# Memory-augmented segment attention with a routed MLP: another layout for the left rows' outputs, and their x loaded at another place

## The chip, the cores and the metric

One Trainium2 chip, one of its cores. The metric is the device time in microseconds of one launch. The core has a matrix engine (TensorE, "PE" in the profile, its weight loads "PEld"), VectorE (DVE), ScalarE (ACT), GpSimd (POOL) and SyncE (SP). SP issues the streamed weights; GpSimd issues the small transfers.

## The reference

What is computed, cut to what matters (2048 rows of 1024, 32 heads of 128, 8 memory rows, 64 segments of 32 rows):

```python
xn = _layernorm(A_x)
mem = A_mem0
for s in range(64):
    h = concat([mem, xn[:, s*32:(s+1)*32]])            # 8 + 32 = 40 rows
    q, k, v = h @ Wq, h @ Wk, h @ Wv                   # 32 heads of 128
    p = softmax(where(mask, q @ k.T * scale, -1e9))    # memory columns, or causal
    o = (p @ v) @ Wo
    mem = o[:, :8]                                     # goes to the next segment
    outs.append(o[:, 8:])
out = x + concat(outs) + B(xn)                         # B: xn plus a gated MLP on 2 routed rows
```

Each segment needs the memory of the one before, so the 64 segments run one after the other.

## The kernel before, in words

**Rows.** A segment has 40 rows: 8 memory rows and 32 of x. The 32-row "main" tile holds the first 24 rows of x and the 8 memory rows. The last 8 rows of x of each segment, the **left rows**, do not depend on the memory, so four segments' left rows (a group of 32) are projected together, one group ahead, in "passes" that use a weight block while it is in SBUF for the main rows. `PASSES` and `COPIES` say by hand in which segment of four (j = s mod 4), phase and step each pass and each copy of a finished unit stands; the unit "o" (the left rows' output projection, tile WL) runs from phase 6 of j = 3 into the start of the next j = 0.

**A segment.** Six phases p of eight steps kc (query, key, query, key of the two halves of 16 heads, then the two halves of the values), each with four matmuls a step (line 780); then 16 steps w of the output projection (`project`, line 578). `hook(p, kc, f)` puts f behind step (p, kc); hooks of one step run in the order in which they were registered, and the copies of `COPIES` are registered first. The order of instructions on each engine is that of the program (`manual_schedule`). `transposes` turns queries and keys and makes QT and KT (lines 633 to 640), `scores` (lines 643 to 663), `exponent` and `soften` (lines 667 to 683) do the softmax of a half, `attend` (lines 686 to 708) multiplies with the values and copies the main rows' result to OT (line 706) and the left rows' to OTL (line 708).

**Weights.** 44 of the 64 blocks of 512 KB stay in SBUF; 20 are streamed each segment through five slots (line 356). A slot is given back when the block's last use in the segment is issued.

**OTL.** One tile a group, [128, 4 segments, 8 rows, 32 heads]. While j is under 3, its part for j = 3 also serves as the zero-filled scratch of the softmax of the left rows (`zeros_and_left`, cleared by `clear_pl`, line 721, on GpSimd). For j = 3 the scratch is the first half of the 512-wide buffer with the tag "bx".

**The left rows' x** is needed twice, loaded by `load_left` (line 323, four transfers of 16 KB on GpSimd's queue). In j = 0 it is loaded for the next group at (3,0) into OTL's part 1, normalised at (5,3) (`norm_left`, line 328) and turned at w = 8. In j = 3 it is loaded for this group at (2,0) into the second half of "bx", made into x + xn at (3,6) (`sum_left`, lines 330 to 337) and added by TensorE at the start of unit "o" (line 556).

**Other users of the tags.** "bx" also holds a block brought back from PSUM (`bring_back(0)`, w = 11, used in phase 0), the left rows' result OL (`copy_unit`, line 598, stored by line 601) and their queries and keys on the way to DRAM; "vl1" holds the left rows' values of the second half.

**GpSimd's queue** in a segment: four stores of the segment before (line 853), the clearing of the scratch, four loads of the next segment's x (`load_seg`, line 275, at (2,0)), in j = 0 four stores of OL, in j = 0 and 3 four loads of left rows, one load of the left rows' queries and keys (line 485, w = 9).

Of the kernel before, what the change touches and what calls it, by code (L numbers as in the profile page):

```python
# [8 lines left out]
BF16 = mybir.dt.bfloat16  # L9
# [43 lines left out]
def kernel(  # L53
# [219 lines left out]
    def load_seg(s):  # L273
        for g in range(4):
            nc.gpsimd.dma_start(out=X[s % 2][32 * g:32 * g + XM, :],  # L275
                                in_=x2[s * SEG:s * SEG + XM, 256 * g:256 * (g + 1)])
# [43 lines left out]
    def load_left(G, t):  # L320
        o4 = x2[4 * G * SEG:4 * (G + 1) * SEG, :].rearrange("(s r) d -> s r d", s=4)
        for g in range(4):
            nc.gpsimd.dma_start(out=t[32 * g:32 * (g + 1), :], in_=o4[:, XM:SEG, 256 * g:256 * (g + 1)])  # L323
        return t
# [185 lines left out]

    def left_out():
        if "otl" not in group:
            group["otl"] = one.tile([P, 4, XL, H], BF16, tag="otl", name="OTL")
        return group["otl"]

    VL = {}
# [63 lines left out]
                                 stop=(last and hs == 1), tile_position=(0, 32 * g), skip_group_check=True)  # L580

    def lhs_left(h):
        return otl_of[0][:, :, :, h].rearrange("p s r -> p (s r)")

    xl_of, otl_of = [None], [None]

    def copy_unit(u, s, engine):
        PS, n = units.pop(u)
        assert n == 0, (u, s, n)
        Gu = group_of(u, s)  # L590
        copy = nc.scalar.copy if engine == "scalar" else nc.vector.tensor_copy
        half = int(u[-1]) if u != "o" else 0
        if u[0] == "v":
            VL[half] = one.tile([P, 512], BF16, tag=f"vl{half}", name="VL")
            copy(out=VL[half][:, :], in_=PS[:, :])
        elif u == "o":
            OL = one.tile([P, 256], BF16, tag="bx", name="OL")
            copy(out=OL[:, :], in_=PS[:, 0:256])
            o4 = out2[4 * Gu * SEG:4 * (Gu + 1) * SEG, :].rearrange("(s r) d -> s r d", s=4)
            for g in range(4):  # L600
                nc.gpsimd.dma_start(out=o4[:, XM:SEG, 256 * g:256 * (g + 1)], in_=OL[32 * g:32 * (g + 1), :])
        else:
            XBl = one.tile([P, 512], BF16, tag="bx", name="XBl")
            copy(out=XBl[:, :], in_=PS[:, :])
            stores.append(lambda: nc.scalar.dma_start(out=ql_d[Gu][2 * half + "qk".index(u[0])], in_=XBl[:, :]))
            if engine == "scalar":
                stores.pop()()

    for s in range(NSEG):
# [9 lines left out]
        def hook(p, kc, fn):  # L619
            hooks.setdefault((p, kc), []).append(fn)  # L620

        def transposes(mat, half, XB):
            PTq = PTB.rearrange("p (i j r) -> p i j r", i=4, j=4)
            for il in range(4):
                nc.tensor.transpose(out=PTq[:, il, :, :].rearrange("p j r -> p (j r)"), in_=XB[:, il * P:(il + 1) * P],  # L625
                                    identity=IDENT[:, :])
            pv = PTq.rearrange("p i j r -> p (i j) r")
            with_left = s > 0 and mat == 0 and half == 0
            if with_left:
                turn_lx()  # L630
            if mat == 0:
                QT[half] = one.tile([P, 16, 32], BF16, tag="bE", name="QT")
                nc.scalar.copy(out=QT[half][:, :, :], in_=pv)  # L633
                if with_left:
                    new_qkl()
            else:
                KT[half] = one.tile([P, 16, NK], BF16, tag="kt", name="KT")
                nc.scalar.copy(out=KT[half].rearrange("p (i q) k -> p i q k", i=4)[:, :, :, 32:NK],
                               in_=qkl[0][:, :, 2 * half + 1, :, :])
                nc.vector.tensor_copy(out=KT[half][:, :, 0:32], in_=pv)  # L640

        def scores(half):
            QKL = qkl[0]
# [25 lines left out]
        def soften(half):  # L669
            S8 = SPS.rearrange("p i a k -> p (i a) k")  # L670
            DN = one.tile([P, 8], F32, tag="nm", name="DN")
            nc.vector.tensor_reduce(out=DN[:, :], in_=S8, axis=AX.X, op=ALU.add)
            nc.vector.reciprocal(out=DN[:, :], in_=DN[:, :])
            PT2 = one.tile([P, 2, 4, 64], BF16, tag=("bA", "bE")[half], name="PT2")
            PTm, PTl = PT2[:, 0], PT2[:, 1]
            PM = PTl.rearrange("p i q -> p (i q)").rearrange("p (b k) -> p b k", b=8)
            PLt = zeros_and_left().rearrange("p (b k) -> p b k", b=8)
            dnb = DN[:, :].unsqueeze(2)
            nc.vector.tensor_tensor(out=PM, in0=S8[:, :, 0:32], in1=dnb.to_broadcast([P, 8, 32]), op=ALU.mult)
            nc.vector.tensor_tensor(out=PLt[:, :, XL * j:XL * (j + 1)], in0=S8[:, :, 32:NK],  # L680
                                    in1=dnb.to_broadcast([P, 8, XL]), op=ALU.mult)
            nc.vector.transpose(out=PTm.rearrange("p i q -> p (i q)"), in_=PM.rearrange("p b k -> p (b k)"))
            nc.vector.transpose(out=PTl.rearrange("p i q -> p (i q)"), in_=PLt.rearrange("p b k -> p (b k)"))
            PTs[half] = (PTm, PTl)

        def attend(half, ph, turn_too=None):
            if half not in OT:
                OT[half] = one.tile([P, 4, 4, SEG], BF16, tag=("kt", "bC")[half], name="OT")
                if half == 0:
                    nxt["wo"] = psA.tile([P, 512], F32, tag="acc", name="WO")  # L690
                sums[half] = [BS[:, 0:4 * NK] if half else nxt["wo"][:, 256:256 + 4 * NK], OPB]
            PTm, PTl = PTs[half]
            for il in range(4):
                for jl in range(2):
                    q0 = 32 * (2 * ph + jl)
                    o = sums[half][jl][:, il * NK:(il + 1) * NK]
                    nc.tensor.matmul(o, lhsT=VM[half][q0:q0 + 32, il * P:(il + 1) * P], rhs=PTm[q0:q0 + 32, il, 0:NK],  # L697
                                     start=True, stop=False, tile_position=(q0, 0), skip_group_check=True)
                    nc.tensor.matmul(o, lhsT=VL[half][q0:q0 + 32, il * P:(il + 1) * P], rhs=PTl[q0:q0 + 32, il, 0:NK],
                                     start=False, stop=True, tile_position=(q0, 0), skip_group_check=True)  # L700
            if turn_too is not None:
                turn_too()
            for jl in range(2):
                ov = sums[half][jl].rearrange("p (i q) -> p i q", i=4)
                copy = nc.scalar.copy if half == 0 or jl == 0 else nc.vector.tensor_copy
                copy(out=OT[half][:, 2 * ph + jl, :, :], in_=ov[:, :, 0:SEG])
                h0 = 16 * half + 8 * ph + 4 * jl
                copy(out=left_out()[:, j, :, h0:h0 + 4].rearrange("p r i -> p i r"), in_=ov[:, :, SEG:NK])

        def zeros_and_left():
            return nxt["bx"][:, 0:256] if j == 3 else left_out()[:, 3].rearrange("p r h -> p (r h)")

        def clear_pl():
            if j == 3:
                nxt["bx"] = one.tile([P, 512], BF16, tag="bx", name="BX")
            z = zeros_and_left()
            if j in (1, 2):
                z = z.rearrange("p (b k) -> p b k", b=8)[:, :, XL * (j - 1):XL * j]  # L720
            nc.gpsimd.memset(z, 0.0)

        def get_left():
            if j == 3:
                nxt["xl"] = load_left(G, nxt["bx"][:, 256:512])
            else:
                nxt["xl"] = load_left(G + 1, left_out()[:, 1].rearrange("p r h -> p (r h)"))

        def prep_left():
            if j == 0:  # L730
# [28 lines left out]
        hook(3, 4, exponent)  # L759
        hook(3, 4, lambda: soften(0))  # L760
        if s + 1 < NSEG:
            hook(2, 0, lambda: load_seg(s + 1))
        if j == 3 or (j == 0 and G + 1 < NT):
            hook(4 if s == 0 else 2 if j else 3, 0, get_left)
            hook(*((3, 6) if j == 3 else (5, 3)), prep_left)
        hook(4, 6, lambda: scores(1))
        hook(5, 0, exponent)
        hook(5, 0, lambda: soften(1))
# [3 lines left out]
        for p, (mat, half) in enumerate(PHASES):  # L772
# [24 lines left out]
            if mat < 2:  # L797
# [2 lines left out]
                hooks.setdefault((p + 1, 3), []).insert(0, lambda m=mat, h=half, b=XB: transposes(m, h, b))  # L800

                if s == 0:
                    XBl = (left_out()[:, 1:3].rearrange("p s r h -> p (s r h)") if mat == 0 else
                           one.tile([P, 512], BF16, tag=("bA", "vl1")[half], name="XBl")[:, :])
                    nc.scalar.copy(out=XBl, in_=PSl[:, :])
                    hooks[p + 1, 3].insert(0, lambda m=mat, h=half, b=XBl: turn_first(m, h, b))
                    nc.gpsimd.dma_start(out=ql_d[0][2 * half + mat], in_=XBl)
# [170 lines left out]
```

## Time and profile before

| | |
|---|---|
| median of 3 runs | 1936.07 us (1923.14 to 1949.76) |
| the profiled execution, time | 1945.1 us |
| the profiled execution, span | 1943.5 us |
| busy: PE, PEld, DVE, ACT, POOL | 1595.4, 891.1, 898.0, 700.3, 440.5 us |
| moved by DMA | 712.42 MB, mean 367 GB/s |
| streamed weights | 1134 transfers of 512 KB, 63 of 256 KB |

How to read the rows: a group's row gives line, engine, operation, what it writes and reads with shapes, the count, then busy us and mean ns of one, then the engine's idle time just before and what ended it. A row of the timeline gives start and duration in us, engine, line, operation, count, and in brackets the idle time before it and what ended that. A row of windows gives the stretch, its length, each engine's busy time with its instructions, the granted TensorE clock (1.00 is full speed), the mean busy share of the 16 DMA engines (packets of a queue can overlap, so it can pass 1) and GB/s. The view of one line lists what its engine waited for in front of it: total us, times.

### The profile page before, as it was taken

The page shows a single profiled execution, that of the slowest core. Times are in us where ns is not written, and L with a number is a line of the kernel's source. Part 1 is how long each engine was busy: PE and PEld are TensorE (multiplying, and loading weights), DVE is VectorE, ACT ScalarE, POOL GpSimd, SP SyncE. Part 2 cuts the span into 40 slices and gives each one's busy share as a digit, 9 for nine tenths or more (in the row PEclk, how much of TensorE's full clock was granted, in tenths as well). Part 3 has the DMA queues.
Part 4 walks back from the last instruction along what each step waited for, and adds up shares of the span by engine and source line. Part 5 has one row for each costly group of instructions (what it writes and reads, how often), then busy time and mean ns, then how long its engine had stood idle before and what let it go on. Part 6 is the DMA issues. An engine that isn't in the chain of part 4 may idle for free.

```text
span 1943.5 us, 82642 instructions
## 1 busy us (share of the span) xinstructions
PE 1595.4 (82%) x36064; PEld 891.1 (46%) x36064; DVE 898.0 (46%) x2880; ACT 700.3 (36%) x1901; POOL 440.5 (23%) x882
## 2 busy tenths in 40 slices
PE   3558898889889888988888888988988888888764
PEld 1224544444454444545454444545444444544443
DVE  6734544454445444544454354445534544454430
ACT  1123343333334343434333343333433343343320
POOL 3202213112221311222121222222122122212120
PEclk8769999999999999999999999999999999999995
DMA  9999999999999999999999999999999999999998
GB/s 370 407 359 381 353 387 355 361 356 335 379 348 384 352 380 359 378 378 365 381 355 369 328 376 377 360 378 354 384 328 380 363 368 388 346 384 358 376 388 335
DMA packets 232123, 712.42 MB, mean 367 GB/s; under 512 B 39296, under 2 KB 53168, under 8 KB 231760
## 3 DMA queue, kind: packets, MB, share of 16 engines
q1 hardware_dynamic: 194384, 671.18, 91.6%
q0 software_dynamic: 28736, 28.09, 4.5%
q10 hardware_dynamic: 8640, 7.87, 1.2%
q8 instruction: 282, 4.62, 0.9%
q14 instruction: 81, 0.66, 0.1%
HBM read 694.32 MB, written 22.29 MB: 369 GB/s over the span
## 4 chain that ended last, share of the span: by engine, by line
DMA 49%; PE 33%; DVE 6%; issue 5%; POOL 4%; ACT 1%; SPq 1%; POOLq 0%; DVEq 0%; ACTq 0%
DMA g<-wsc 33%; PE PSm L780 16%; PE WO L578 5%; DMA ql_d<-XBl 4%; DMA BX<-in_A_x_dram 4%; PE PSl L571 3%; PE WL L578 3%; PE BT L625 2%; DMA XP<-in_A_x_dram 2%; POOL X L275 2%; POOL BX L323 1%; POOL out_dram L853 1%; DMA MW<-in_B_w_gate_dram 1%; DVE XR L250 1%; DMA MW<-in_B_w_up_dram 1%
## 5 line engine op out<-in xcount | busy, mean ns | idle before, releaser
L780 PE MATMUL PSm<-wres,ST 128*32 128x512 bf16 x8448 | 726.7, 389 | 12.4 <-DVE ST L318 5.8
L780 PEld LDWEIGHTS <-ST 128*32 128x32 bf16 x12288 | 328.1, 97 | 385.1 <-issue 158.8
L780 PE MATMUL PSm<-g,ST 128*32 128x512 bf16 x3588 | 365.9, 392 | 81.1 <-DMA g<-wsc 62.1
L578 PEld LDWEIGHTS <-OT 128*32 128x32 bf16 x8192 | 219.0, 98 | 150.6 <-issue 132.8
L799 ACT CAST XB<-PSm 128x512 bf16<-128x512 f32 x256 | 150.2, 587 | 308.2 <-PE PSm L780 305.2
L578 PE MATMUL WO<-wres,OT 128*32 128x256 bf16 x5632 | 241.7, 279 | 21.6 <-DMA wres<-in_A_Wo_dram 8.6
L485 POOL DMA_DIRECT2D LX<-ql_d x63 | 33.5, 532 | 869.5 <-PE WO L578 368.0
L571 PE MATMUL PSl<-wres,STL 128*32 128x512 bf16 x2112 | 203.9, 390 | 0.7 <-issue 0.6
L578 PE MATMUL WO<-g,OT 128*32 128x256 bf16 x2560 | 134.9, 282 | 67.9 <-DMA g<-wsc 54.8
L853 POOL DMA_DIRECT2D out_dram<-X x256 | 129.1, 513 | 259.2 <-DVE X L851 253.6
L275 POOL DMA_DIRECT2D X<-in_A_x_dram x256 | 128.8, 507 | 227.0 <-DMA out_dram<-X 86.8
L640 DVE COPY KT<-BT 128x512 bf16<-128x512 bf16 x128 | 52.4, 410 | 276.4 <-ACT XB L799 110.3
L810 ACT CAST VM<-PSm 128x512 bf16<-128x512 f32 x128 | 77.9, 609 | 149.3 <-PE PSm L780 149.3
L379 ACT COPY BK<-KEPT 128x512 bf16<-128x512 bf16 x126 | 74.3, 590 | 133.1 <-issue 131.3
L633 ACT COPY QT<-BT 128x512 bf16<-128x512 bf16 x128 | 74.9, 585 | 118.8 <-PE BT L492 69.6
L571 PEld LDWEIGHTS <-STL 128*32 128x32 bf16 x3072 | 85.3, 98 | 57.5 <-issue 8.9
L383 DVE COPY g<-KEPT 128x512 bf16<-128x512 bf16 x126 | 47.6, 420 | 135.6 <-PE PSm L780 86.7
L625 PEld LDWEIGHTS <-XB 128*128 128x128 bf16 x1024 | 58.5, 98 | 106.9 <-ACT XB L799 63.7
L697 PEld LDWEIGHTS <-VM 32*128 32x128 bf16 x2048 | 67.5, 91 | 84.1 <-issue 72.0
L379 DVE COPY BK<-KEPT 128x512 bf16<-128x512 bf16 x126 | 54.7, 434 | 106.6 <-DMA ql_d<-XBl 78.7
L625 PE MATMUL BT<-IDENT,XB 128*128 128x128 bf16 x1024 | 102.2, 222 | 2.0 <-ACT QKL L504 1.4
L657 DVE TENSOR_TENSOR BS<-BS,CT 128x96 f32<-128x96 f32 (+1 forms) x256 | 59.7, 233 | 90.1 <-PE BS L650 85.7
(173 smaller groups left out, 2422.8 us busy)
## 6 DMA issues: line engine op xcount, KB each, us to landing
g<-wsc SPq DMA_DIRECT2D x1134, 512.0 KB, 6.2
g<-wsc SPq DMA_DIRECT2D x63, 256.0 KB, 5.2
LX<-ql_d POOLq DMA_DIRECT2D x63, 128.0 KB, 5.9
ql_d<-XBl ACTq DMA_DIRECT2D x60, 128.0 KB, 5.8
MW<-in_B_w_gate_dram SPq DMA_DIRECT2D x16, 448.0 KB, 9.4
MW<-in_B_w_up_dram SPq DMA_DIRECT2D x16, 448.0 KB, 9.0
wres<-in_A_Wk_dram SPq DMA_DIRECT2D x12, 512.0 KB, 11.7
MW<-in_B_w_down_dram SPq DMA_DIRECT2D x12, 512.0 KB, 10.1
```

Of the source, the lines that this page charges most:

```text
L275: nc.gpsimd.dma_start(out=X[s % 2][32 * g:32 * g + XM, :], in_=x2[s * SEG:s * SEG + XM, 256 * g:256 * (g + 1)])
L379: copy(out=back[c][:, :], in_=KEPT_COLS[KEPT_WHOLE][c])
L571: nc.tensor.matmul(PSl[32 * jq:32 * jq + 32, :], lhsT=STL[:, g % KC, :], rhs=part(Gv, jq), start=first_, stop=last_, tile_position=(0, 32 ...
L578: nc.tensor.matmul(PS[32 * g:32 * g + 32, 0:256], lhsT=lhs(h), rhs=Gv[:, D * hs + 256 * g:D * hs + 256 * (g + 1)], start=(first and hs == ...
L625: nc.tensor.transpose(out=PTq[:, il, :, :].rearrange("p j r -> p (j r)"), in_=XB[:, il * P:(il + 1) * P], identity=IDENT[:, :])
L633: nc.scalar.copy(out=QT[half][:, :, :], in_=pv)
L657: nc.vector.tensor_tensor(out=S4, in0=S4, in1=m, op=ALU.add)
L697: nc.tensor.matmul(o, lhsT=VM[half][q0:q0 + 32, il * P:(il + 1) * P], rhs=PTm[q0:q0 + 32, il, 0:NK], start=True, stop=False, tile_position ...
L780: nc.tensor.matmul(PSm[32 * jq:32 * jq + 32, :], lhsT=ST[:, kc, :], rhs=part(Gv, jq), start=(kc == 0), stop=(kc == KC - 1), tile_position= ...
L799: nc.scalar.copy(out=XB[:, :], in_=PSm[:, :])
L810: nc.scalar.copy(out=VM[half][:, :], in_=PSm[:, :])
L853: nc.gpsimd.dma_start(out=out2[s * SEG:s * SEG + XM, 256 * g:256 * (g + 1)], in_=OB[32 * g:32 * g + XM, :])
```

## The change

* OTL becomes [128, 32 heads, 4 segments, 8 rows]: for each head the 32 left rows of the group lie side by side. The copies of line 708 now write runs of eight elements instead of single elements 64 bytes apart, the weights of the left output projection become contiguous, and the scratch of the softmax lies in pieces of eight elements (contiguous still for j = 3).
* In j = 3 the left rows' x is loaded at (1,1) instead of (2,0) and summed at (4,5) instead of (3,6). In j = 0 it is loaded at (3,1) instead of (3,0), in the first segment at (4,1) instead of (4,0).
* `load_seg` moves from (2,0) to (2,4), which in j = 0 is behind the stores of OL.
* In j = 0 the left rows' x goes to a tile of "bx"; OL goes to "vl1", but for the last segment.
* In j = 0 ScalarE instead of VectorE copies the second half's keys.
* In the first segment the left rows' queries take the "bx" buffer.

```diff
-            group["otl"] = one.tile([P, 4, XL, H], BF16, tag="otl", name="OTL")
+            group["otl"] = one.tile([P, H, 4, XL], BF16, tag="otl", name="OTL")
...
-        return otl_of[0][:, :, :, h].rearrange("p s r -> p (s r)")
+        return otl_of[0][:, h, :, :].rearrange("p s r -> p (s r)")
...
-            OL = one.tile([P, 256], BF16, tag="bx", name="OL")
+            OL = one.tile([P, 256], BF16, tag="bx" if s == NSEG - 1 else "vl1", name="OL")
...
-                nc.vector.tensor_copy(out=KT[half][:, :, 0:32], in_=pv)
+                (nc.scalar.copy if j == 0 and half else nc.vector.tensor_copy)(out=KT[half][:, :, 0:32], in_=pv)
...
-            PLt = zeros_and_left().rearrange("p (b k) -> p b k", b=8)
+            PLt = zeros_and_left()
...
-            nc.vector.tensor_tensor(out=PLt[:, :, XL * j:XL * (j + 1)], in0=S8[:, :, 32:NK],
+            nc.vector.tensor_tensor(out=PLt[:, :, j, :], in0=S8[:, :, 32:NK],
...
-            nc.vector.transpose(out=PTl.rearrange("p i q -> p (i q)"), in_=PLt.rearrange("p b k -> p (b k)"))
+            nc.vector.transpose(out=PTl.rearrange("p i q -> p (i q)"), in_=PLt.rearrange("p b s r -> p (b s) r"))
...
-                copy(out=left_out()[:, j, :, h0:h0 + 4].rearrange("p r i -> p i r"), in_=ov[:, :, SEG:NK])
+                copy(out=left_out()[:, h0:h0 + 4, j, :], in_=ov[:, :, SEG:NK])
...
-            return nxt["bx"][:, 0:256] if j == 3 else left_out()[:, 3].rearrange("p r h -> p (r h)")
+
+            z = nxt["bx"][:, 0:256].rearrange("p (h r) -> p h r", r=XL) if j == 3 else left_out()[:, :, 3, :]
+            return z.rearrange("p (b s) r -> p b s r", s=4)
...
-            if j in (1, 2):
-                z = z.rearrange("p (b k) -> p b k", b=8)[:, :, XL * (j - 1):XL * j]
-            nc.gpsimd.memset(z, 0.0)
+            nc.gpsimd.memset(z[:, :, j - 1, :] if j in (1, 2) else z, 0.0)
...
-                nxt["xl"] = load_left(G + 1, left_out()[:, 1].rearrange("p r h -> p (r h)"))
+                nxt["xl"] = load_left(G + 1, one.tile([P, 256], BF16, tag="bx", name="XL")[:, :])
...
-            hook(2, 0, lambda: load_seg(s + 1))
+            hook(2, 4, lambda: load_seg(s + 1))
         if j == 3 or (j == 0 and G + 1 < NT):
-            hook(4 if s == 0 else 2 if j else 3, 0, get_left)
-            hook(*((3, 6) if j == 3 else (5, 3)), prep_left)
+            hook(4 if s == 0 else 1 if j else 3, 1, get_left)
+            hook(*((4, 5) if j == 3 else (5, 3)), prep_left)
...
-                    XBl = (left_out()[:, 1:3].rearrange("p s r h -> p (s r h)") if mat == 0 else
-                           one.tile([P, 512], BF16, tag=("bA", "vl1")[half], name="XBl")[:, :])
+                    XBl = one.tile([P, 512], BF16, tag="bx" if mat == 0 else ("bA", "vl1")[half], name="XBl")[:, :]
```

## The prediction

> **What bounds the kernel now.** I read the page first (span, transfer queues, chain), then the length and the transfer share of the four kinds of segment, then the groups of instructions that wait, then two single segments in order of time. A group is four segments, j = 0 to 3; "left rows" are the eight last rows of each segment.
>
> ```profile
> span 1943.5 us, 82642 instructions
> ...
> q1 hardware_dynamic: 194384, 671.18, 91.6%
> ...
> DMA 49%; PE 33%; DVE 6%; issue 5%; POOL 4%; ACT 1%; SPq 1%; POOLq 0%; DVEq 0%; ACTq 0%
> ```
>
> The queue of the streamed weights alone fills 91.6% of the sixteen engines' span, and half of the last chain is transfers. So an instruction taken away is worth nothing where the transfers run without a break; only places where they break off can give time. The next fence is the busy time in windows, one sum for each kind of segment, in the order j = 0 (15 segments), 1 (15), 2 (14), 3 (14).
>
> ```profile
> sum 416.80, PE 362.07 PEld 212.43 DVE 193.78 ACT 170.25 POOL 141.57; mean PE 24.14 PEld 14.16 DVE 12.92 ACT 11.35 POOL 9.44
> ...
> sum 405.10, PE 359.34 PEld 191.91 DVE 192.68 ACT 162.08 POOL 71.01; mean PE 23.96 PEld 12.79 DVE 12.85 ACT 10.81 POOL 4.73
> ...
> sum 382.70, PE 331.37 PEld 176.00 DVE 180.38 ACT 149.64 POOL 65.74; mean PE 23.67 PEld 12.57 DVE 12.88 ACT 10.69 POOL 4.70
> ...
> sum 413.20, PE 347.14 PEld 201.78 DVE 185.14 ACT 144.91 POOL 100.82; mean PE 24.80 PEld 14.41 DVE 13.22 ACT 10.35 POOL 7.20
> ```
>
> That is 27.8, 27.0, 27.3 and 29.5 us a segment: j = 3 is over 2 us longer than j = 1 with nearly the same TensorE work. The timeline of one j = 3 segment (it starts at 965.1) shows why, and the windows view shows the price.
>
> ```profile
> 967.85 0.31 POOL L721 MEMSET BX<- 128x256 bf16 x1
> ...
> 973.86 2.35 POOL L323 DMA_DIRECT2D BX<-in_A_x_dram  x4
> ...
> 982.04 0.34 DVE L337 TENSOR_SCALAR BX<-BX,RI 128x256 bf16<-128x256 bf16 x1 [2.86 <-DMA BX<-in_A_x_dram]
> ...
> 982.77 0.21 PE L648 MATMUL BS<-KT,QT 128*32 128x40 bf16 x4 [2.89 <-DVE KT L640]
> ```
> ```profile
> 979.50:982.80 3.30, 0.41 (x12) 0.03 (x6) 0.68 (x2) 0.00 (x0) 0.00 (x0) 1.00 1.02 390
> 982.80:986.30 3.50, 2.96 (x86) 1.68 (x87) 2.36 (x7) 1.69 (x6) 0.00 (x0) 1.00 0.71 229
> ```
>
> VectorE stands 2.86 us for the left rows' x (line 337), the second half's keys stand behind it, and TensorE waits 2.89 us for them. Transfers go on through the stall (share 1.02) until all five slots are full; then they run at 0.71 for 3.5 us, about 1.0 us lost.
>
> **The change part by part.** *The j = 3 load.* Its four issues go ahead of the next segment's four x loads and follow the memset directly: from 973.86 to about 968.2 in this segment. They land 5.7 us after issue.
>
> ```profile
> BX<-in_A_x_dram POOLq DMA_DIRECT2D x64, 16.0 KB, 5.7
> out_dram<-OL POOLq DMA_DIRECT2D x64, 16.0 KB, 5.8
> ```
>
> The last issue then starts near 970.0 and lands near 975.7, some 6 us before it did, while the sum now comes later, between the keys' copy and the second scores. The x loads that go behind it are wanted only near the segment's end. What disappears:
>
> ```profile
> L648 PE MATMUL BS<-KT,QT 128*32 128x40 bf16 x2048 | 50.0, 182 | 35.6 <-DVE KT L640 34.6 <-issue 0.5
> ...
> L337 DVE TENSOR_SCALAR BX<-BX,RI 128x256 bf16<-128x256 bf16 x16 | 5.5, 346 | 28.7 <-DMA BX<-in_A_x_dram 28.6
> ```
>
> So 28.6 us of VectorE's waiting, and at most 34.6 of TensorE's (that row has other waits for keys too); I take 28. After two such stalls the granted clock fell to half:
>
> ```profile
> 311.80:315.20 3.40, 3.40 (x74) 1.45 (x59) 2.41 (x7) 1.01 (x2) 0.00 (x0) 0.50 0.68 235
> 424.50:427.90 3.40, 2.87 (x60) 1.28 (x60) 2.19 (x7) 1.01 (x2) 0.00 (x0) 0.50 0.53 182
> ```
>
> Half speed for 3.4 us is at most 1.7 us; three such groups would be 5, so TensorE gets back up to 33. But the end moves at least by the transfers' lost time: 0.29 x 3.5 = 1.0 us in the segment above, 0.32 x 3.4 = 1.1 and 0.47 x 3.4 = 1.6 in these two. At 1.3 in sixteen groups that is 21 us. Bounds 16 to 33; I take **-21**, since j = 1 and 2 already run with the transfers unbroken and would hold any surplus.
>
> *The j = 0 load.* Here the order of the queue turns against the change. Segment 32 (starts at 994.7):
>
> ```profile
> 1001.63 0.51 POOL L275 DMA_DIRECT2D X<-in_A_x_dram  x1 [4.21 <-PE PSm L780]
> ...
> 1004.19 2.40 POOL L601 DMA_DIRECT2D out_dram<-OL  x4
> ...
> 1007.51 1.16 POOL L323 DMA_DIRECT2D OTL<-in_A_x_dram  x2 [0.26 <-DMA X<-in_A_x_dram]
> 1008.86 0.58 POOL L323 DMA_DIRECT2D OTL<-in_A_x_dram  x1 [0.18 <-DVE KT L640]
> ...
> 1003.12 0.37 ACT L598 CAST OL<-WL 128x256 bf16<-128x256 f32 x1
> ...
> 1014.26 0.34 DVE L328 TENSOR_SCALAR OTL<-OTL,RI 128x256 bf16<-128x256 bf16 x1 [0.41 <-DMA OTL<-in_A_x_dram]
> ...
> 1015.54 0.35 DVE L288 TENSOR_SCALAR X<-X,RI 128x256 bf16<-128x256 bf16 x1
> ...
> 1017.15 0.29 DVE L706 CAST OT<-BT 128x128 bf16<-128x128 f32 x1 [1.27 <-PE BT L699]
> ```
> ```profile
>   DMA X<-in_A_x_dram: 5.7, 9
> ```
>
> The last fence is from the view of line 323: nine times the left rows' load waited for the landing of an x load, with which it shares no tile. In the order four x loads, four stores, four left loads, the x load of the same number stands eight issues ahead; so GpSimd's transfers seem to share eight completion semaphores. The x loads now move from (2,0) to (2,4), behind the stores of OL. Then the issue eight ahead of each left load is a store of OL, which is young. Worked out here: stores from 1003.55 (line 598 ends at 1003.49) to 1005.95, x loads to 1008.0, first store landed at 1003.55 + 5.8 = 1009.35, so the left loads issue from 1009.6, one every 0.6, the last at 1011.4 instead of 1008.86, and it lands near 1017.2 instead of 1014.2. Lines 328 to 288 take 1014.26 to 1015.89, that is 1.63; they end at 1018.9. Behind them on VectorE stands the second half's output copy, which began at 1017.15: 1.8 late, and TensorE's next attend needs the bank that it empties. Fifteen groups at 1.8 are 27 us of stall, and nothing at the other end. What hides it:
>
> ```profile
> PE PSm L780 <- DMA g<-wsc: 62.1, 132, 1.8
> ...
> PE WO L578 <- DMA g<-wsc: 54.8, 106, 2.3
> ```
>
> TensorE waits 116.9 us for streamed weights, 1.9 a segment; a TensorE that is late skips the next such waits, while five empty slots keep the transfers running. So I charge a third: **+9** (bounds 0 to 27).
>
> The Trainium skill, "DMA: Bandwidth & Descriptors", section Anatomy of one DMA (gpsimd path), fits 2.0 us plus bytes / 436e3, about 2.04 us for 16 KB. By it the stores would have landed before the left loads' turn, the slip would be nothing, and the sum 9 us lower; the rows' 5.7 and 5.8 us speak against it.
>
> *Output copies.* The left part of each attend copy writes single elements 64 bytes apart; now runs of eight.
>
> ```profile
> L708 ACT CAST OTL<-BT 128x32 bf16<-128x32 f32 x128 | 40.6, 317 | 0.0
> ...
> L504 ACT COPY QKL<-BT 128x128 bf16<-128x128 bf16 x4 | 1.1, 265 | 34.3 <-PE BT L503 34.3
> ```
>
> A copy of four times the size in runs of eight takes 265, so 50 ns and perhaps twice that are saved on each. At most three stand in line before TensorE goes on: 0.15 to 0.3 us a segment, 9 to 19 us over 63; transfers hide it in j = 1 and 2 and most of the rest. I take **-3** (0 to -19).
>
> *Keys on ScalarE (j = 0, second half).* In the same segment:
>
> ```profile
> 1007.50 0.30 ACT L638 COPY KT<-QKL 128x128 bf16<-128x128 bf16 x1 [0.69 <-PE BT L625]
> ...
> 1008.30 0.38 DVE L640 COPY KT<-BT 128x512 bf16<-128x512 bf16 x1
> ...
> L633 ACT COPY QT<-BT 128x512 bf16<-128x512 bf16 x128 | 74.9, 585 | 118.8 <-PE BT L492 69.6 <-PE BT L625 48.0 <-DVE BS L663 1.1
> ```
>
> VectorE comes to it at 1008.30 after the softmax and ends at 1008.68; ScalarE would go from 1007.80 to 1008.39, 0.3 sooner. Where VectorE is free it would end 0.3 + 0.585 - 0.38 = 0.5 later. Fifteen times: -5 to +7; **-1**.
>
> *Edits at nothing.* The weight loads of the left outputs become contiguous, but the pace is the matmuls': below, a left piece takes 0.22 (989.70 to 989.92) and the main one ahead of it 0.23. OL in another buffer: its last store lands near 1011.2 in segment 32, and the tag is wanted again by line 595 at 1015.33, 4 us later; without that cover ScalarE would wait there. The softmax's transposes and memsets now take pieces of eight; no row shows a transpose of that form. Its bounds are the 445 ns that it has (nothing), and, if every piece cost what a scattered write does, about 0.8 us more, on 96 of them, hidden by a VectorE that is under half busy: up to +10. I take nothing.
>
> ```profile
> 1015.33 0.60 ACT L595 CAST VL<-PSl 128x512 bf16<-128x512 f32 x1
> ...
> 989.47 0.40 PE L578 MATMUL WO<-g,OT 128*32 128x256 bf16 x8
> 989.70 0.39 PE L578 MATMUL WL<-g,OTL 128*32 128x256 bf16 x8
> 989.78 0.31 ACT L708 CAST OTL<-BS 128x32 bf16<-128x32 f32 x1
> 989.92 0.39 PE L578 MATMUL WO<-wres,OT 128*32 128x256 bf16 x8
> ```
>
> **Sum:** -21 + 9 - 3 - 1 = -16 us on the profiled execution's own 1945.1, so 1929. The median of the runs, 1936.07, is 0.9954 of that execution; the forecast is 1920.
>
> **Rivals.** *B, the full gain.* The j = 0 slip doesn't come or stays in VectorE's slack: 1945.1 - 25 = 1920, times 0.9954 is 1911; and where TensorE's 33 us all count, with 6 from the copies, 1945.1 - 39 = 1906 gives 1897, which I name for it. For it: transfers also fall below full share after the stall, so TensorE, not they, sets the pace there. Against it: 1.26 us of slack (1015.89 to 1017.15) against a slip of 3. The Trainium skill's fit, named above, would have it come out as B's 1911.
>
> *C, hidden anyway.* The chain is half transfers; what j = 3 gains, j = 0 gives back in waits for weights: 1936. Against it: the share of 0.53 to 0.71 after the stalls.
>
> *D, the other side.* The j = 0 slip decides as soon as the left rows land over 1.3 us later than now. If TensorE cannot make it up, all 27 us count, and half clock after seven of the stalls (1.7 each) adds 12; the j = 3 gain is held to 16 by the transfers: +23, so 1968, times 0.9954 is 1959. For it: the segment's tail, where the stall falls, has little work to run ahead with.
>
> *E, it isn't what it says.* The segments' outputs now lie interleaved in one tile. If the program ordered them by extent and not by element, ScalarE's output copies would wait for VectorE's second softmax. If that took as much as the 1.8 us above, in 47 segments, it were 85 us; half of it hidden, and the gains with it, leaves 1987, times 0.9954 is 1978. Against it: the matmul at 989.70 above reads interleaved columns while the copy at 989.78 writes their neighbours; nobody waits.
>
> **How the numbers follow.** Forecast 0.52, B 0.20, C 0.13, D 0.10, E 0.05. Two per cent, about what a measurement of this kernel can tell from no change, is 39 us: under 1897 or over 1975. Half of B and a little of the forecast's tail, with the spread of the medians, give faster 0.20; E and the tail of D give slower 0.09; 0.71 is left. The range goes from B's 1897, less 4 for the spread of the runs, to just short of D: 1893 to 1955. The forecast's own range is 1903 to 1940.
>
> **What would show it.** Right: no wait at line 337's successor for the left rows' x, second scores in j = 3 not waiting for keys, transfers near 1.0 between 17 and 21 us of those segments, j = 3 near 28 us. Then, in j = 0, the left rows' load issued 2 to 3 us later, waits of it for the landing of the stores of OL, VectorE standing at line 328's successor for 2 us or more in most groups, but j = 0 longer by less than 1 us. Wrong: if j = 0 grows as much as j = 3 shrinks (C, D), if the left copies or transposes come out longer, or if ScalarE's output copies wait for VectorE (E).

## The result, and the profile after

The changed kernel takes 1944.87 us (median of 20 runs, 1940.29 to 1957.3), the kernel before 1937.99 in runs beside it (20 runs): a ratio of 1.0054 [1.0032, 1.0076], some 10 us **slower**, where 16 us of gain were forecast. (The ratio is taken from runs made side by side and is not the quotient of the two medians, which lie 7 us apart; microseconds given below for whole kernels come from such ratios.) Its profiled execution has 1949.07 us. The page's lines on the span and the weights' queue:

```profile
span 1947.4 us, 82580 instructions
...
q1 hardware_dynamic: 194384, 671.18, 91.2%
```

The windows of the segments, one sum for each of j = 0 (15 segments), 1 (15), 2 (14), 3 (14), as in the prediction:

```profile
sum 445.00, PE 375.78 PEld 215.39 DVE 185.50 ACT 169.81 POOL 143.08; mean PE 25.05 PEld 14.36 DVE 12.37 ACT 11.32 POOL 9.54
...
sum 401.70, PE 354.04 PEld 189.97 DVE 190.26 ACT 155.12 POOL 71.17; mean PE 23.60 PEld 12.66 DVE 12.68 ACT 10.34 POOL 4.74
...
sum 379.10, PE 333.11 PEld 176.29 DVE 178.66 ACT 142.49 POOL 65.96; mean PE 23.79 PEld 12.59 DVE 12.76 ACT 10.18 POOL 4.71
...
sum 397.20, PE 343.35 PEld 199.59 DVE 184.49 ACT 138.54 POOL 100.72; mean PE 24.52 PEld 14.26 DVE 13.18 ACT 9.90 POOL 7.19
```

Against 416.80, 405.10, 382.70 and 413.20 before, j = 3 is 16 us shorter (1.14 a segment, so 18 in 16 groups), j = 1 and 2 together 7 shorter, and **j = 0 28 us longer**. The groups of instructions, shapes kept apart:

```profile
L648 PE MATMUL BS<-KT,QT 128*32 128x40 bf16 x2048 | 50.3, 181 | 5.3 <-DVE KT L640 2.8 <-ACT KT L640 1.6 <-DVE RI L270 0.4
...
L337 DVE TENSOR_SCALAR BX<-BX,RI 128x256 bf16<-128x256 bf16 x16 | 5.5, 347 | 0.9
L328 DVE TENSOR_SCALAR XL<-XL,RI 128x256 bf16<-128x256 bf16 x16 | 5.5, 346 | 67.1 <-DMA XL<-in_A_x_dram 67.1
...
L697 PE MATMUL BS<-PT,VM 32*128 32x40 bf16 x512 | 45.5, 181 | 35.6 <-DVE RI L270 35.6
...
L708 ACT CAST OTL<-BT 128x32 bf16<-128x32 f32 x128 | 27.9, 218 | 0.0
...
L683 DVE STREAM_TRANSPOSE PT<-OTL 128x256 bf16<-128x256 bf16 x96 | 42.7, 445 | 5.6
...
L640 ACT COPY KT<-BT 128x512 bf16<-128x512 bf16 x16 | 9.3, 580 | 0.0
```

The two waits of j = 3 are gone: line 337 waits for no load (28.6 us before) and the second scores hardly wait for keys (2.8 against 34.6). In their place stand 67.1 us of VectorE at line 328, before the left rows' load of j = 0, and 35.6 us of TensorE at line 697, which waits for "RI L270", a reciprocal on VectorE. The view of waits says what held the load back, and what the waits for weights did:

```profile
POOL XL L323 <- DMA out_dram<-OL: 24.5, 18, 2.4
...
PE WO L578 <- DMA g<-wsc: 59.7, 116, 2.3
...
PE PSm L780 <- DMA g<-wsc: 54.5, 123, 1.7
```

The left rows' issues wait for the landing of stores of OL, another tile and another direction, as the prediction worked out. The timeline of one j = 0 segment (it starts at 1562.4) shows the whole chain:

```profile
1571.22 2.41 POOL L601 DMA_DIRECT2D out_dram<-OL  x4 [1.02 <-ACT OL L598]
...
1573.62 2.08 POOL L275 DMA_DIRECT2D X<-in_A_x_dram  x4
...
1577.12 0.62 POOL L323 DMA_DIRECT2D XL<-in_A_x_dram  x1 [1.42 <-DMA out_dram<-OL]
...
1578.57 1.75 POOL L323 DMA_DIRECT2D XL<-in_A_x_dram  x3 [0.84 <-DMA out_dram<-OL]
...
1586.53 0.35 DVE L328 TENSOR_SCALAR XL<-XL,RI 128x256 bf16<-128x256 bf16 x1 [5.63 <-DMA XL<-in_A_x_dram]
...
1586.98 0.16 DVE L270 RECIPROCAL RI<-BS 128x1 f32<-128x1 f32 x1
...
1587.19 0.18 PE L697 MATMUL BS<-PT,VM 32*128 32x40 bf16 x1 [3.96 <-DVE RI L270]
```

Line 270 belongs to `norm_seg`, which stands behind the left rows' norm on VectorE. It reads the row statistics MR, and MR lies in columns 320 and up of the tile BS (`MR = BS[:, 320:...]`), whose columns 0 to 159 attend(1,0) writes. So TensorE stands at w = 5 until VectorE, which waits for a load, has read two columns. This is called the hold below. What comes behind is in the windows of the same segment, and, for a shorter stall, of segment 16:

```profile
1582.50:1586.50 4.00, 0.73 (x24) 0.54 (x21) 0.00 (x0) 0.28 (x1) 0.00 (x0) 0.90 1.04 377
1586.50:1590.00 3.50, 2.81 (x64) 1.88 (x67) 1.81 (x10) 0.71 (x4) 0.00 (x0) 0.50 0.62 214
1590.00:1592.60 2.60, 2.60 (x56) 1.92 (x56) 1.14 (x4) 1.08 (x3) 0.54 (x1) 0.51 0.81 247
...
566.40:568.60 2.20, 0.02 (x2) 0.02 (x2) 0.62 (x4) 0.00 (x0) 0.00 (x0) 0.98 1.02 386
568.60:571.90 3.30, 3.30 (x74) 2.21 (x77) 1.71 (x9) 0.74 (x5) 0.51 (x1) 0.50 0.97 362
```

With each of the two stalls the granted clock falls to half. By the trace's clock records it is half for 61.4 us in j = 0 (18 stretches of 3.41 us; 13 of the 15 segments), against 10.2 us before. And behind the longer stall transfers fall to 0.62 and 0.81: in the trace no weight transfer is issued from 1582.84 to 1588.24, which fits slots that are all full while TensorE, held and then at half speed, gives none back.

### The profile page after: what moved, and what is told of

The parts are those of the page before. It is cut to its first block, busy times and chain, and to the rows that moved or that the text cites. A ratio compares the mean times of both kernels' runs of the same rounds, so it can differ in the third digit from the quotient of the medians.

```text
span 1947.4 us, 82580 instructions
## 1 busy us (share of the span) xinstructions
PE 1600.4 (82%) x36064; PEld 888.8 (46%) x36064; DVE 883.7 (45%) x2864; ACT 677.0 (35%) x1917; POOL 442.1 (23%) x882
## 5 line engine op out<-in xcount | busy, mean ns | idle before, releaser
L578 PE MATMUL WO<-wres,OT 128*32 128x256 bf16 x5632 | 251.2, 288 | 20.6 <-issue 10.7
L578 PE MATMUL WO<-g,OT 128*32 128x256 bf16 x2560 | 139.1, 294 | 75.8 <-DMA g<-wsc 59.7
L640 DVE COPY KT<-BT 128x512 bf16<-128x512 bf16 x112 | 46.3, 414 | 276.4 <-ACT XB L799 112.6
L706 ACT CAST OT<-BS 128x128 bf16<-128x128 f32 x128 | 34.1, 266 | 210.7 <-PE BT L699 135.6
## 6 DMA issues: line engine op xcount, KB each, us to landing
MW<-in_B_w_down_dram SPq DMA_DIRECT2D x12, 512.0 KB, 10.2
```

What stands on the lines that cost most here:

```text
L578: nc.tensor.matmul(PS[32 * g:32 * g + 32, 0:256], lhsT=lhs(h), rhs=Gv[:, D * hs + 256 * g:D * hs + 256 * (g + 1)], start=(first and hs == ...
```

## The experiments

The three main parts were taken one at a time. In each diff the side with "+" is the kernel that ran; ratios are to the kernel before, run beside it.

**The x load put back, all else as changed.**

```diff
-            hook(2, 4, lambda: load_seg(s + 1))
+            hook(2, 0, lambda: load_seg(s + 1))
```

> The changed kernel with one line undone: the next segment's x loads go back from (2,4) to (2,0). Theory Q (the queue): in j = 0 the x loads moved behind the stores of OL, so the left rows' load is issued later and waits for those stores' landing, VectorE stands at the left rows' norm, TensorE behind it, and the granted clock falls. Then the j = 0 segments (29.9 us in the changed kernel, 27.9 before) go back to about 27.9, VectorE's wait for XL falls from 67 to about 10 us, j = 3 keeps its 28.4: about 1915 to 1920 us, 0.988 to 0.992 of before. Rival P (another part: the layout, the buffers, the keys on ScalarE): the loss stays, 1940 to 1945 us, 1.001 to 1.005.

1915.86 against 1940.64 us: 0.987 [0.9832, 0.9908]. The j = 0 windows and the waits:

```profile
sum 408.60, PE 355.91 PEld 206.30 DVE 186.48 ACT 169.91 POOL 140.78; mean PE 23.73 PEld 13.75 DVE 12.43 ACT 11.33 POOL 9.39
```
```profile
PE WO L578 <- DMA g<-wsc: 71.2, 151, 1.8
...
PE PSm L780 <- DMA g<-wsc: 65.2, 135, 2.3
...
DVE XL L328 <- DMA XL<-in_A_x_dram: 18.1, 11, 3.9
...
PE BS L697 <- DVE RI L270: 2.6, 3, 1.9
```

With the load four steps sooner the hold at line 697 goes, j = 0 is 36 us shorter than in the changed kernel, and no stretch of half clock is left in j = 0. The place of `load_seg` costs 1.0054 - 0.987 = 0.018, 36 us. (A difference of two ratios, here and below, is uncertain by 7 to 9 us.)

**The x load alone moved,** in the kernel before and in j = 0 alone.

```diff
-            hook(2, 0, lambda: load_seg(s + 1))
+            hook(2, 0 if j else 4, lambda: load_seg(s + 1))
```

> The kernel before with one line changed: in j = 0 alone the next segment's x loads go from (2,0) to (2,4), behind the stores of OL. Theory Q: this alone brings the loss: j = 0 from 27.9 to about 29.9 us, VectorE's wait for the left rows' x from 9 to over 60 us, 15 groups x 2 = 30 us, about 1.013 to 1.017 of before. Rival P: within 5 us of before, 0.997 to 1.003.

1967.9 us, 1.0165 [1.0123, 1.0206]: +32 us. The waits show the same chain in the old layout and the old tiles:

```profile
DVE OTL L328 <- DMA OTL<-in_A_x_dram: 58.1, 14, 6.7
...
PE WO L578 <- DMA g<-wsc: 48.3, 88, 1.6
...
PE PSm L780 <- DMA g<-wsc: 45.6, 97, 1.4
...
PE BS L697 <- DVE RI L270: 37.5, 14, 6.2
...
POOL OTL L323 <- DMA out_dram<-OL: 21.2, 25, 1.9
```

**The left rows' load of j = 3 alone,** in the kernel before.

```diff
-            hook(4 if s == 0 else 2 if j else 3, 0, get_left)
-            hook(*((3, 6) if j == 3 else (5, 3)), prep_left)
+            hook(*((4, 0) if s == 0 else (1, 1) if j else (3, 0)), get_left)
+            hook(*((4, 5) if j == 3 else (5, 3)), prep_left)
```

> The kernel before with the j = 3 part of the change alone: the left rows' x is loaded at (1,1) instead of (2,0) and summed at (4,5) instead of (3,6). Theory Q: the gain in j = 3 stands by itself, 1.1 to 1.5 us in 16 segments, 18 to 24 us, 0.988 to 0.991 of before. Rival C (the transfers give it back in the next segments anyway): 0.997 to 1.000, with j = 0 longer by as much as j = 3 is shorter.

1917.7 us, 0.9882 [0.985, 0.9914]: -23 us. The j = 3 windows, 413.20 before:

```profile
sum 396.40, PE 345.57 PEld 203.21 DVE 186.21 ACT 145.46 POOL 100.43; mean PE 24.68 PEld 14.52 DVE 13.30 ACT 10.39 POOL 7.17
```

**The layout alone** (with the new buffers): the changed kernel with every place and the keys as before.

```diff
-                (nc.scalar.copy if j == 0 and half else nc.vector.tensor_copy)(out=KT[half][:, :, 0:32], in_=pv)
+                nc.vector.tensor_copy(out=KT[half][:, :, 0:32], in_=pv)
...
-            hook(2, 4, lambda: load_seg(s + 1))
+            hook(2, 0, lambda: load_seg(s + 1))
...
-            hook(4 if s == 0 else 1 if j else 3, 1, get_left)
-            hook(*((4, 5) if j == 3 else (5, 3)), prep_left)
+            hook(4 if s == 0 else 2 if j else 3, 0, get_left)
+            hook(*((3, 6) if j == 3 else (5, 3)), prep_left)
```

> The changed kernel with all places as before (x loads at (2,0), left rows' load at (2,0) and (3,0), sum at (3,6), keys on VectorE): what is left is the layout of the left outputs and the other buffers. The copies of line 708 take 0.19 to 0.22 us in the changed kernel where they took 0.29 to 0.32. Theory (off the path, hidden by the transfers): 0.996 to 1.001 of before, j = 3 still 29.5 us. Rival (the copies are on the path of every segment's end): 0.3 us in 63 segments, 0.990 or less.

1942.65 against 1941.97 us, 0.9997 [0.9963, 1.003]. Copies of 218 ns instead of 317 are worth nothing that shows. The three parts add up within their uncertainty: -23 + 32 + 0 = +9, and the whole change has +10.

**Which block holds TensorE?** First, the left rows' norm of j = 0 moved behind attend(1,0), the load as late as ever:

```diff
-            hook(*((4, 5) if j == 3 else (5, 3)), prep_left)
+            if j == 3:
+                hook(4, 5, prep_left)
...
+            if w == 7 and j == 0 and G + 1 < NT:
+                prep_left()
```

> The changed kernel with the left rows' norm in j = 0 moved on VectorE from (5,3) to step w = 7 of the output projection, behind the next segment's norm and the output copies of attend(1,0). The late load stays as late as it is. Theory Q1 (what costs is that VectorE's later work stands behind the wait): TensorE's wait of 35.6 us for attend(1,1) goes, most of the 30 us come back, 0.990 to 0.996 of before. Rival Q2 (the load lands too late for the turn at w = 8 itself): the stall stays at w = 8, 1.001 to 1.006.

1919.1 us, 0.9906 [0.9873, 0.994]. The hold at line 697 is gone, 7.7 us of waiting for the left rows at their turning are left. But this edit takes both the statistics' read and the output copies out from behind the norm. So, in another kernel, the norm stands behind `norm_seg` (which reads the statistics) but still ahead of attend(1,0), whose copies remain behind it:

```diff
-            hook(*((4, 5) if j == 3 else (5, 3)), prep_left)
+            if j == 3:
+                hook(4, 5, prep_left)
...
             xn = norm_seg(s + 1)
+            if j == 0 and G + 1 < NT:
+                prep_left()
```

> The changed kernel with the left rows' norm in j = 0 behind the next segment's norm on VectorE, but still ahead of attend(1,0)'s output copies. The load is as late as it is. Theory Q3 (TensorE is held at w = 5 because VectorE reads the row statistics from the PSUM bank that attend(1,0) writes, and that read stands behind the wait): the wait for line 270 goes; what is left is a shorter one at w = 8, for the copies, about half: 0.996 to 1.002 of before. Theory Q4 (my prediction's: the copies of attend(1,0) are what TensorE waits for): nothing changes, 1.003 to 1.008.

1924.08 against 1939.69 us, 0.9932 [0.9903, 0.9962], faster than either side expected. The waits:

```profile
DVE XL L328 <- DMA XL<-in_A_x_dram: 39.5, 15, 3.8
...
POOL XL L323 <- DMA out_dram<-OL: 23.3, 18, 2.5
...
PE BT L697 <- DVE OTL L708: 10.4, 11, 2.5
...
PE BS L697 <- DVE RI L270: 2.3, 2, 1.8
```

The load comes as late as before (23.3 of waits for stores), VectorE still waits 39.5 us, but TensorE's hold falls from 35.6 to 2.3 us, and 1.0054 - 0.9932 = 0.012, 24 us, of the 36 come back. The order of the reads decided most of it. What is left, some 12 us, goes with a wait that the changed kernel did not have: 11 times in j = 0 TensorE now stands for VectorE's output copies (line 708), 10.4 us in all. So the copies come second: they hold TensorE once the read no longer does. Only moving the norm behind them as well, in the kernel ahead of this one, takes that wait away too.

**Is the half clock a part of the loss?** Nine matmuls that nobody reads were put ahead of an attend in j = 0, to keep TensorE busy while it is held. The first try put them at w = 8:

```diff
+            if w == 8 and j == 0 and 0 < s and G + 1 < NT:
+                WARM = psL.tile([P, 512], F32, tag="accl", name="WARM")
+                for _ in range(9):
+                    nc.tensor.matmul(WARM[:, :], lhsT=IDENT[:, :], rhs=res_tiles[0][:, 0:512], start=True, stop=True)
```

> The changed kernel with work added: in j = 0, in front of attend(1,1) at w = 8, nine matmuls of 128x128 by 128x512 that nobody reads, about 1.9 us at full clock in 15 groups, 29 us of TensorE work. They stand where TensorE waits 35.6 us in all for VectorE. Theory K (a good part of the loss is the clock that falls to half after the stall: 13 of the 15 j = 0 segments had such a stretch in their tail, 58 us in all): with the stall filled the clock stays up, j = 0 gets shorter by 0.5 to 1.5 us though work was added, 0.993 to 1.002 of before. Rival S (the stall itself is all): no shorter than the changed kernel, 1.004 to 1.015 of before.

1968.84 against 1941.97 us, 1.0134 [1.01, 1.0169]; half clock in j = 0 54.6 us, the hold unchanged at 35.7. It says nothing of the clock: the hold is at w = 5, so these matmuls stand behind it and only add work. This miss is what showed the place of the hold. With the same nine matmuls ahead of attend(1,0), at w = 5:

```diff
             if w == 5:
+                if j == 0 and 0 < s and G + 1 < NT:
+                    WARM = psL.tile([P, 512], F32, tag="accl", name="WARM")
+                    for _ in range(9):
+                        nc.tensor.matmul(WARM[:, :], lhsT=IDENT[:, :], rhs=res_tiles[0][:, 0:512], start=True, stop=True)
                 attend(1, 0)
```

> The changed kernel with the nine unread matmuls (about 1.9 us at full clock) in front of attend(1,0) at w = 5 in j = 0, where the changed kernel's trace has the wait of 35.6 us (TensorE for VectorE's read of the row statistics, line 270). With them at w = 8 they came behind that wait and could not fill it. Theory K (the clock that falls after the stall is a good part of the loss): the wait shrinks to about 10 us, the half-clock time in j = 0 (61 us in the changed kernel) to under 25, and j = 0 gets 0.4 to 1.2 us shorter though work was added: 0.996 to 1.002 of before. Rival S (the stall's length is all): j = 0 as long as in the changed kernel or longer, 1.003 to 1.010.

1940.1 against 1939.69 us, 1.001 [0.998, 1.004]. One of its j = 0 windows, with their sum, then its waits:

```profile
1542.60:1569.70 27.10, 25.49 (x587) 15.84 (x579) 12.34 (x43) 11.37 (x33) 9.64 (x18) 1.00 0.98 366
...
sum 416.90, PE 382.54 PEld 216.74 DVE 184.55 ACT 170.20 POOL 142.57; mean PE 25.50 PEld 14.45 DVE 12.30 ACT 11.35 POOL 9.51
```
```profile
DVE XL L328 <- DMA XL<-in_A_x_dram: 65.7, 15, 6.0
...
PE BS L697 <- DVE RI L270: 8.6, 8, 2.2
```

The left rows land as late as ever (65.7), and 27 us of work are added (14 groups, since the first and the last have none, x 9 matmuls x 0.216 us from one to the next), as much as TensorE's wait shrinks (35.6 to 8.6). TensorE is kept from its own work as long as before, and still the kernel is no slower, by the ratios rather faster (1.001 against 1.0054; the intervals overlap by a little): half clock in j = 0 falls from 61.4 to 3.4 us, and the window shown has 1.00. So a part of the loss was the clock. How large a part is not settled: 0.0044, 8 us, by the ratios; 28 us by the j = 0 sums of the profiled executions, of which this kernel's (1925.75) was 14 us under its median.

**The stores out of GpSimd's queue:** OL stored by ScalarE.

```diff
-                nc.gpsimd.dma_start(out=o4[:, XM:SEG, 256 * g:256 * (g + 1)], in_=OL[32 * g:32 * (g + 1), :])
+                nc.scalar.dma_start(out=o4[:, XM:SEG, 256 * g:256 * (g + 1)], in_=OL[32 * g:32 * (g + 1), :])
```

> The changed kernel with the four stores of OL issued by ScalarE instead of GpSimd. The x loads stay at (2,4) and the left rows' load behind them. Theory Q with eight shared semaphores: the store eight ahead of a left load is then a store of the segment before, long landed, and 2.4 us of issues are out of the way: no wait of XL's load for OL's landing (24.5 us in the changed kernel), left rows landed by about 18 us of the segment, j = 0 near 27.4, 0.986 to 0.991 of before (ScalarE has 4 x 0.33 us more in 15 groups). Rival (moving the x loads hurts in itself): 1.000 to 1.005.

1941.52 against 1941.97 us, 0.9998 [0.997, 1.0026]: a miss. The late load is cured, but not the time:

```profile
ACT XB L799 <- DMA out_dram<-OL: 43.0, 15, 3.3
...
PE BT L625 <- ACT XB L799: 29.0, 15, 2.5
...
DVE XL L328 <- DMA XL<-in_A_x_dram: 4.0, 2, 3.7
```

The stores no longer stand eight issues ahead of the left loads, and the wait of 67.1 is 4.0. But each group of four stores now holds ScalarE for 2.9 us in front of its next copy of queries or keys, and TensorE waits 29.0 us for that copy, a wait that the changed kernel did not have.

**The left rows' load first.** In j = 0 it goes to (1,1), ahead of all:

```diff
-            hook(4 if s == 0 else 1 if j else 3, 1, get_left)
+            hook(4 if s == 0 else 1, 1, get_left)
```

> The changed kernel with the left rows' load of j = 0 at (1,1) instead of (3,1): the buffer is free there, since OL has another one. It goes ahead of the stores of OL and of the x loads. Theory Q: the left rows land by about 11 us of the segment, VectorE never waits for them, j = 0 at 27.0 to 27.3, the x loads' landing (about 18 us) is still ahead of the norm at 20: 0.983 to 0.988 of before, at least as fast as the kernel with the x loads put back. Rival (the x loads behind OL are late themselves): VectorE waits at line 286 for X instead, 0.992 to 1.003.

1919.32 us, 0.9865 [0.9822, 0.9909]. The waits for stores are gone, as are those at lines 328 (but for the first, 3.6) and 697. Together with the x load put back:

> The changed kernel with the left rows' load of j = 0 at (1,1) and the x loads back at (2,0): both ahead of the stores of OL. Theory Q: no wait for left rows or x anywhere in j = 0, no better than the kernels that have one of the two, 0.983 to 0.989 of before, j = 0 at 27.0 to 27.4. Rival (a last wait in j = 0 is left in those): 0.980 or less.

1914.95 us, 0.9862 [0.9816, 0.9909], no better than either alone: once the left rows land in time, how early is worth nothing that shows.

## Why the prediction was wrong

**j = 3, -21: right,** with its mechanism. Alone it has -23 us (0.9882; -29 to -17), and the bounds of 16 to 33 held. In the j = 3 windows TensorE's waits for keys go (26.6 us), while its waits for weights rise from 8.6 to 16.9: the transfers kept a part back, as the step assumed. Its three stalls with half clock were too few, though: 11 stretches of it began in those windows before, 7 with this edit.

**The order of GpSimd's queue: right.** The eighth-issue rule was inferred from nine waits; the load slipped by about 3 us, from landing 20.5 us into the segment to 23.8, and waited for stores of OL. In all 800 issues of GpSimd no transfer starts before the landing of the one eight ahead, and the smallest distance is 0.28 us; 81 start before the landing of the one seven ahead.

**j = 0, "so I charge a third: +9": wrong,** and this step turned the sign. By the one-edit comparison with the x load put back it is +36, by the single edit +32. Its reason was that a late TensorE "skips the next such waits" for weights. That happened: counted in the j = 0 windows alone, those waits are 16.7 us against 32.8 with the load put back, so 16 us were hidden, near the 18 that the step allowed. What failed is the amount from which they are taken. The step put it at 27 us of stall. The runs show 33 us of hold at line 697 (35.6 - 2.6) and, on top, TensorE busy 20 us longer with the same matmuls (375.78 against 355.91 in the j = 0 windows), as 61.4 us of a clock at half speed can make it. 33 + 20 - 16 is 37, and the windows differ by 36 (445.0 - 408.6).

Two things were missed in that amount. The first blocker was named wrongly: not the second half's output copies, behind all of lines 328 to 288, but line 270's read, five instructions sooner, at w = 5. The slack is then shorter, and the hold is 2.5 us (35.6 / 14) instead of 1.8. The waits of before could have told, for the same wait stands there, short and twice:

```profile
PE BS L697 <- DVE RI L270: 1.8, 2, 1.2
```

Line 270 writes RI from BS, and BS is the tile that line 697 writes.

The other thing is the half clock. It had been seen, after stalls of under 3 us in j = 3, but was charged only to rival D (seven stalls, 12 us), not to the forecast, which had the same stalls. Rival D, "the other side" (TensorE cannot make the slip up), is thus nearest in mechanism: it put 39 us on j = 0. It missed in holding j = 3 to 16 us. The measured 1945 lies outside the forecast's own range of 1903 to 1940; that it lies within the wide one, 1893 to 1955, says little, since no change at all would lie there too. Rival C is nearest in number (1936), but not in mechanism: j = 0 did not give the gain back in waits for weights, which fell there.

The Trainium skill, "TensorE: Matmul & The Clock Gate", part 1, says that activity is judged in free-running windows of about 3.4 us and that idle gaps above that length cost the clock. The trace agrees on the length (each stretch of half clock is 3.41 us or a multiple) but not on the gap: the window above had 2.20 us without work and then 0.50. By the page's rule most of these holds (11 of the 14 are shorter than 3.4 us) would have kept full speed; the measurement decides.

**Copies, -3: nothing** (0.9997; -7 to +6 us). The time of a copy fell by a third, and TensorE's waits for it, small before, nearly went:

```profile
PE WO L578 <- ACT OTL L708: 7.4, 37, 0.2
...
PE WO L697 <- ACT OTL L708: 4.2, 9, 0.6
```

Of these 11.6 us of before, 3.2 are left with the layout alone; the 8 us do not show in its time. **Keys, -1:** not run alone; the changed kernel with the x load put back (0.987) is within the noise of the j = 3 edit and the layout together (0.9882 x 0.9997 = 0.9879). **Edits at nothing:** the transposes take 445 ns as before, OL's new buffer brings no wait. **Rival E** did not come: ScalarE's output copies wait for no softmax.

## What to carry to other kernels

Before a load moves past others on a shared queue, find the earlier issue whose landing it has to wait for (here the one eight ahead), and ask how old that one is then. For a wait made later, look behind the waiting instruction for the first thing that another engine needs, a small read from a tile that the other engine writes too, not for the largest. Where the clock behaves as here, a stall of TensorE of two microseconds is to be priced twice, once as it is and once as half speed behind it, and one such load in the wrong place can cost more than a good change elsewhere brings: here the two differ by one line, and without it the kernel is 1.3% faster than before.

## What the runs showed of the hardware that was not expected

The clock fell to half after holds of about 2 us (2.20 us idle, then 0.50), and 27 us of matmuls that nobody reads, put into the hold, kept it at full speed in j = 0 but for one stretch of 3.4 us, and cost nothing net. Four store issues moved to ScalarE hold it 2.9 us (43.0 / 15), so a queue that looks free is not a free place. GpSimd's transfers never start before the landing of the one eight ahead (0.28 us at the least). And TensorE waits for VectorE's read of other columns of the same PSUM tile; whether the program's tracking by tile or the bank asks for it, no run here told apart.
